# One fused kernel, a TensorE product shared by two blocks on row halves, and a new order of its steps

## The chip, the cores and the metric

The kernel runs on one core of one Trainium2 chip. The metric is the device time of one execution in microseconds (us). TensorE (PE) does the matmuls, and its weight loads are shown apart (PEld); VectorE (DVE), ScalarE (ACT) and GpSimd (POOL) do the elementwise work; SyncE (SP) issues the transfers.

## The reference, cut to what matters

Three layers follow one another: an mLSTM-like attention over gates (2 batches, 8 heads, 768 rows, head size 40), a mixture of four attention experts, and a mixer. The change touches mostly the last stage of the mixer, which is called the channel stage here:

```
xt = x.transpose(0, 2, 1)
h = np.maximum(xt @ w_tok1, 0.0) @ w_tok2
u = x + h.transpose(0, 2, 1)
h2 = np.maximum(u @ w_ch1, 0.0) @ w_ch2      # 320 -> 1536 -> 320
return (u + h2).astype(np.float32)
```

## The kernel before

All three layers are one program. The work is cut into parts, Python generators that stop at each step; `ORDER` is a list of numbers written out ahead, and each number runs the next step of one part on one engine (part number times 5 plus the engine: PE, ACT, DVE, POOL, SP). So the order of every engine's queue is that list; a negative number -n puts n small filler matmuls on PE (`fillers`, tile `still`). The conditions that a part yields (`on(...)`) are checked when the list is played at build time; on the chip an engine waits only where data or a buffer needs it.

Gates are scanned along the sequence on DVE, then each of 12 chunks (2 batches of 6) of 128 rows goes through `m_rows` (a tile `rt` of stabiliser rows), `m_products` (tag pd), `m_whole` (scores, 40-row products), `m_scores`, `m_carry`, `m_intra`, `m_update`. The first two chunks' `rt` are made by a multiply (four ACT operations or one on DVE); from the third on two small DMAs fill them. Then come the experts (`p_qk`, `p_v`, `a_scores`, `a_unit`, `a_value`, `a_tail`), the token stage (`t_hidden`, `t_mix`, `c_turn`) and the channel stage.

Every product that needs precision is a sum of hi and lo halves in fp32r. In the channel stage the 320 inputs are two blocks of 128 rows and one of 64 that stands twice, on rows 0 to 63 and 64 to 127. `c_hidden(k, g)`, for 12 blocks k of 128 hidden columns and 3 groups g of 512 rows, runs `kpass`: three products for each of the first two blocks and two for the third, eight of 128x512 in all, into one PSUM bank. In the third block the hi weights stand on the upper rows and their lo part on the lower, so hi times x_hi and lo times x_hi are one product; the eighth is the same weights by x_lo. ACT then writes h hi (relu), DVE h lo, both into tiles of the tag `e`, and `c_out(k, g)` runs four times three products of 128x320 into four accumulator banks (tile `cw` is a weight block, `h` its input). There are eight PSUM banks.

Weights of the channel stage come as 64-bit floats: `narrow` loads one (tile `raw`), narrows it with three DVE operations, one ACT operation ahead of them and one behind, and DVE writes the lo half (`cw`). A block k from 6 on can only be loaded when a place (`home`) is free; blocks 8 to 11 take those that `c_out` of blocks 0 to 3 gives back with the last group (`cwused`).

Of the kernel before, what the change touches and what calls it, by code (L numbers as in the profile page):

```python
# [39 lines left out]
EARLY = 4  # L40
STOP = -1000
# [14 lines left out]
    937, 422, 524, 895, 187, 508, 432, 900, STOP, 560, 917, 187, 440, 488, 936, 896, 387, 440, 561, 901, 1482, 530,  # L56
# [1175 lines left out]
```

## Time and profile before

| | us |
|---|---|
| median of 3 runs | 334.23 |
| lowest, highest | 334.22, 334.96 |
| profiled execution: its time | 334.46 |
| its span, first to last instruction | 332.7 |

Some 1.76 us of the profiled execution lie outside the span. Busy time of an engine is the union of its instructions, which overlap: a start-to-start time is shorter than an instruction's own duration. PE's ends are modelled, so short waits of PE can hide in its busy time.

### The profile page before, as it was taken

To read this page: it belongs to the slowest core of one execution; us is meant where nothing else is said; L and a number is where in the kernel's file an instruction comes from. 1 tells how busy PE (TensorE), PEld (TensorE's weight loads), DVE (VectorE), ACT (ScalarE), POOL (GpSimd) and SP (SyncE) were. 2 spreads that over 40 slices of the span, in tenths; PEclk is the share of its full clock that TensorE was granted. 3 is DMA by queue.
4 is the path that set the end of the run, shared out by engine and by line. 5 is a ranking of instruction groups with operands and counts; after the bars stand their busy time and mean duration, and the time that the engine had idled before them with its cause. 6 is when DMAs were issued, how large, how long until landed. Compare 5 with 4: busy or idle time off the path is not lost.

```text
span 332.7 us, 7751 instructions
## 1 busy us (share of the span) xinstructions
PE 326.1 (98%) x3034; PEld 293.8 (88%) x3034; DVE 243.1 (73%) x674; ACT 179.4 (54%) x453; POOL 43.3 (13%) x82
## 2 busy tenths in 40 slices
PE   8999999999989999999999999999999999999995
PEld 7779989898888989988899899999889989889985
DVE  4999999999999999999997636543535886411413
ACT  7997769787938886678685513311213442211110
POOL 4232443031421000011120010000000000000000
PEclk9999999999999999999999999999999999999999
DMA  7962844540300354121011502000101200100302
GB/s 228 394 225 97 304 157 153 216 155 13 144 0 3 128 175 144 49 87 41 2 42 48 164 12 89 0 0 2 47 0 41 87 1 2 39 2 0 104 16 79
DMA packets 10300, 29.05 MB, mean 87 GB/s; under 512 B 1272, under 2 KB 3224, under 8 KB 10264
## 3 DMA queue, kind: packets, MB, share of 16 engines
q1 hardware_dynamic: 10120, 28.54, 24.8%
q8 instruction: 24, 0.39, 0.5%
q14 instruction: 12, 0.10, 0.1%
q10 hardware_dynamic: 144, 0.02, 0.0%
HBM read 26.50 MB, written 1.97 MB: 86 GB/s over the span
## 4 chain that ended last, share of the span: by engine, by line
PE 57%; DVE 32%; ACT 4%; issue 3%; DMA 2%; SPq 0%; POOL 0%; DVEq 0%; POOLq 0%; ACTq 0%
PE bank L195 52%; DVE am L864 3%; PE bank L881 3%; DVE e L587 3%; DVE tf L477 3%; DVE tf L474 2%; DMA gt<-in_dram 2%; DVE cw L219 1%; DVE w L222 1%; DVE tf L472 1%; DVE xt L677 1%; ACT am L870 1%; DVE x L222 1%; PE bank L625 1%; DVE q L763 1%
## 5 line engine op out<-in xcount | busy, mean ns | idle before, releaser
L195 PE MATMUL bank<-ut,cw 128*128 128x512 f32 x288 | 72.4, 395 | 0.0
L195 PE MATMUL bank<-cw,h 128*128 128x320 f32 x432 | 70.6, 310 | 0.0
L195 PEld LDWEIGHTS bank<-cw,h 128*128 128x128 f32 x432 | 66.0, 188 | 2.7 <-issue 0.2
L1044 ACT ACTIVATE h<-bank 128x512 fp32r<-128x512 f32 x36 | 21.6, 600 | 78.4 <-PE bank L195 78.3
L195 PEld LDWEIGHTS bank<-ut,cw 128*128 128x128 f32 x288 | 52.6, 188 | 9.8
L1046 DVE SCALAR_TENSOR_TENSOR h<-bank,h 128x512 fp32r<-128x512 f32 x36 | 24.8, 689 | 48.4 <-ACT h L1044 48.4
L870 ACT ACTIVATE am<-am,mn 128x128 f32<-128x128 f32 (+5 forms) x48 | 32.1, 671 | 11.0 <-DVE mn L867 6.6
L864 DVE CUSTOM_DVE_ANT_0 am<-bank,mk 128x384 f32<-128x384 f32 (+3 forms) x64 | 30.6, 500 | 0.8 <-PE bank L195 0.7
L195 PE MATMUL bank<-xt,wh 128*128 128x256 f32 x144 | 26.6, 290 | 0.0
L881 PE MATMUL bank<-ident,am 128*128 128x128 f32 x168 | 24.8, 275 | 0.0
L195 PE MATMUL bank<-ks,q 64*128 64x384 f32 (+2 forms) x192 | 22.4, 343 | 1.1 <-DVE q L763 1.0
L469 ACT ACTIVATE tf<-raw 128x384 f32<-128x384 f32 (+1 forms) x32 | 17.1, 535 | 11.4 <-DVE cw L219 6.0
L216 ACT COPY atr<-bank 128x384 f32<-128x384 f32 (+3 forms) x53 | 22.2, 442 | 2.0 <-PE bank L881 1.9
L195 PEld LDWEIGHTS bank<-xt,wh 128*128 128x128 f32 x144 | 21.8, 189 | 1.0 <-issue 0.2
L195 PE MATMUL bank<-atr,vg 128*64 128x128 f32 x336 | 22.2, 277 | 0.0
L881 PEld LDWEIGHTS bank<-ident,am 128*128 128x128 f32 x168 | 19.4, 140 | 1.8 <-issue 0.3
L195 PEld LDWEIGHTS bank<-atr,vg 128*64 128x64 f32 x336 | 18.4, 137 | 2.1 <-issue 0.6
L195 PEld LDWEIGHTS bank<-ks,q 64*128 64x128 f32 x192 | 15.8, 185 | 4.9 <-DVE q L763 1.2
L477 DVE SCALAR_TENSOR_TENSOR tf<-raw,minus,tf 128x384 uint32<-128x384 uint32 (+1 forms) x32 | 19.1, 595 | 0.2
L474 DVE SCALAR_TENSOR_TENSOR tf<-raw,tf 128x384 uint32<-128x384 uint32 (+1 forms) x32 | 17.5, 556 | 0.3
L1070 DVE TENSOR_TENSOR u<-bank,u 128x320 f32<-128x320 f32 x24 | 11.0, 486 | 8.5 <-PE bank L195 8.5
L587 DVE TENSOR_TENSOR e<-bank,e 128x512 f32<-128x512 f32 x24 | 16.2, 682 | 0.1
(160 smaller groups left out, 601.5 us busy)
## 6 DMA issues: line engine op xcount, KB each, us to landing
kv<-in_dram SPq DMA_DIRECT2D x11, 848.0 KB
raw<-in_dram SPq DMA_DIRECT2D x20, 384.0 KB
raw<-in_dram SPq DMA_DIRECT2D x13, 320.0 KB
os<-in_dram SPq DMA_DIRECT2D x4, 480.0 KB
out_dram<-u SPq DMA_DIRECT2D x12, 160.0 KB
raw<-in_dram SPq DMA_DIRECT2D x3, 386.0 KB
kv<-in_dram SPq DMA_DIRECT2D x1, 512.0 KB
gt<-in_dram SPq DMA_DIRECT2D x1, 512.0 KB
```

The lines of the kernel that those rows point to most:

```text
L195: PE.matmul(o, lt, r, start=first, stop=last)
L216: (A.copy if e == "A" else V.tensor_copy)(o, i)
L469: A.activation(t, w[:, :, 1].bitcast(F32), AF.Copy, scale=2.0 ** -112)
L474: V.scalar_tensor_tensor(u, w[:, :, 0], 29, u, op0=OP.logical_shift_right, op1=OP.bitwise_or)
L477: V.scalar_tensor_tensor(t.bitcast(U32), w[:, :, 1], minus.bitcast(U32), u, op0=OP.bitwise_and, op1=OP.bitwise_or)
L587: V.tensor_mul(EE[n, u], PS[n][u], EE[n, u])
L864: V.tensor_tensor_reduce(a[:, b0 * 128:b1 * 128], s["p", e, ci], mks, -0.125, 3e38, OP.add, OP.min, s["mn"][:, ci, e:e + 1])
L870: A.activation(a[:, 0:w], a[:, 0:w], AF.Exp, bias=s["mn"][:, z, e:e + 1], scale=-1.0, accum_out=s["sm"][:, 0, e:e + 1])
L881: PE.transpose(pt[:, k - b0], a[:, k * 128:(k + 1) * 128], ident)
L1044: A.activation(h[0], p1, AF.Relu)
L1046: V.scalar_tensor_tensor(h[1], p1, 0.0, f32(h[0]), op0=OP.max, op1=OP.subtract)
L1070: V.tensor_add(uo(b, i), ACC[h, n // 4][n % 4], uo(b, i))
```

## The change

- `c_hidden` keeps seven products. The eighth is left to a new part `c_last`, for two blocks k and k+1 of one group together: one product on rows 0 to 63 for block k, one on rows 64 to 127 for k+1, each into its own bank. For that, `narrow` writes the lo half of an odd block's third part on the upper rows in place of the lower ones. The lo-by-lo term of the third block, which the old eighth product held, falls away.
- relu and the lo half become a part of their own, `c_split`, after `c_last`; its tiles come from the pool `big` in place of `e`.
- `DIRECT = 3`: the third chunk's `rt` is made by a multiply; its copy and its two DMAs fall away, and the fifth chunk, which takes the same buffer, gets the copy.
- `m_products`, `m_whole` and `a_tail` yield other conditions for the order list (no wait on the chip).
- `ORDER` is a new list. As it is read against the parts, it has `c_last` 18 times in nine runs of one to three pairs, 58 fillers in runs of 19, 18, 11, 10 (before 80, of 19, 49, 2, 2, 8), and counted by kind takes 25 steps from DVE and gives it 12 of other engines.

```diff
+DIRECT = 3
...
-        if n > 1 and (n < 4 or c < 2):
+        if n >= DIRECT and (n < DIRECT + 2 or c < 2):
             yield on("AV", "sml", *free)
             copy(plan.eng, rt(n), sel(n, True))
-        if n > 1:
+        if n >= DIRECT:
...
         if rem:
-            sub(plan.eng, hi[64:128, m:], t[64:128, m:], f32(hi[64:128, m:]))
+            low = slice(0, 64) if home[1] % 2 else slice(64, 128)
+            sub(plan.eng, hi[low, m:], t[low, m:], f32(hi[low, m:]))
...
     def c_hidden(k, g):
-        yield on("P", ..., take=["bank", "e", "e"])
+        yield on("P", ..., take=["bank"])
         ws = NAR["c1", k]
-        p1 = bank([128, 512])
-        kpass(p1, lambda w, xx, blk, r: (ws[w][r, 128 * blk:128 * blk + 128], UT[g][xx][r, blk]))
+        P1[k, g] = bank([128, 512])
+        for n, (w, x, blk) in enumerate(((0, 0, 0), (1, 0, 0), (0, 1, 0), (0, 0, 1), (1, 0, 1), (0, 1, 1), (0, 0, 2))):
+            mm(P1[k, g], ws[w][:, 128 * blk:128 * blk + 128], UT[g][x][:, blk], n == 0, False)
+        mark(("hd", k, g))
+
+    def c_last(k, g):
+        yield on("P", ("hd", k, g), ("hd", k + 1, g))
+        for u in range(2):
+            r = slice(64 * u, 64 * u + 64)
+            mm(P1[k + u, g], NAR["c1", k + u][0][r, 256:384], UT[g][1][r, 2], False, True)
...
+    def c_split(k, g):
+        yield on("A", ("hp", k - k % 2, g), take=["big"])
+        p1 = P1[k, g]
+        h = H2[k, g] = two(big([128, 2, 512], F32R, "h2"))
         A.activation(h[0], p1, AF.Relu)
```

## Rows read from the trace of the kernel before

**Rows 1.** The page: span, busy time by engine, shares of the chain that ended last.
```profile
span 332.7 us, 7751 instructions
PE 326.1 (98%) x3034; PEld 293.8 (88%) x3034; DVE 243.1 (73%) x674; ACT 179.4 (54%) x453; POOL 43.3 (13%) x82
...
PE 57%; DVE 32%; ACT 4%; issue 3%; DMA 2%; SPq 0%; POOL 0%; DVEq 0%; POOLq 0%; ACTq 0%
```
**Rows 2.** The chain that ended last: start us, us, what.
```profile
2.17 6.06 DMA gt<-in_dram
...
12.14 0.60 DVE e L587
...
92.43 10.38 PE bank L195 x120
...
164.17 0.41 DVE u L1002
164.63 3.60 PE bank L195 x49
...
235.44 92.53 PE bank L195 x515
328.00 1.81 DVE u L1070 x4
```
**Rows 3.** Stretches of 10 us: busy us per engine (instructions), granted clock, DMA share, GB/s.
```profile
0.00:10.00 10.00, 8.96 (x90) 7.54 (x90) 5.62 (x16) 7.50 (x18) 3.76 (x17) 1.00 0.77 261
...
50.00:60.00 10.00, 9.92 (x138) 9.25 (x139) 9.90 (x29) 8.25 (x22) 3.46 (x6) 1.00 0.53 189
...
150.00:160.00 10.00, 10.00 (x85) 8.80 (x85) 9.82 (x33) 8.86 (x26) 1.34 (x2) 1.00 0.13 34
...
300.00:310.00 10.00, 10.00 (x58) 9.07 (x57) 1.86 (x4) 1.80 (x3) 0.00 (x0) 1.00 0.00 0
```
**Rows 4.** Timeline, PE in the channel stage: start us, us, instruction.
```profile
240.67 2.00 PE L195 MATMUL bank<-ut,cw 128*128 128x512 f32 x8
...
242.51 1.92 PE L195 MATMUL bank<-cw,h 128*128 128x320 f32 x12
...
244.27 2.01 PE L195 MATMUL bank<-ut,cw 128*128 128x512 f32 x8
```
**Rows 5.** Timeline, PE around three runs of row-half pairs; in brackets the idle before.
```profile
66.93 0.80 PE L195 MATMUL bank<-ks,q 64*128 64x384 f32 x6
67.66 1.09 PE L195 MATMUL bank<-atr,vg 128*64 128x128 f32 x16
...
75.53 0.94 PE L195 MATMUL bank<-ks,q 64*128 64x512 f32 x6
76.39 0.79 PE L195 MATMUL bank<-cb,w 128*64 128x82 f32 x16
...
174.97 0.31 PE L195 MATMUL bank<-up,tw 128*128 128x320 f32 x1
175.21 0.19 PEld L195 LDWEIGHTS bank<-ks,q 64*128 64x128 f32 x2 [0.19 <-issue]
175.21 1.31 PE L195 MATMUL bank<-ks,q 64*128 64x384 f32 x12
176.46 0.71 PE L195 MATMUL bank<-up,tw 128*128 128x320 f32 x3
```
**Rows 6.** Groups of DVE by form: xcount | busy us, mean ns | idle before.
```profile
L1046 DVE SCALAR_TENSOR_TENSOR h<-bank,h 128x512 fp32r<-128x512 f32 x36 | 24.8, 689 | 48.4 <-ACT h L1044 48.4
...
L587 DVE TENSOR_TENSOR e<-bank,e 128x512 f32<-128x512 f32 x24 | 16.2, 682 | 0.1
...
L222 DVE TENSOR_TENSOR x<-os,dn 128x320 f32<-128x320 f32 x9 | 5.3, 586 | 0.1
...
L216 DVE CAST ut<-bank 128x384 fp32r<-128x384 f32 x6 | 3.3, 546 | 0.0
L216 DVE COPY u<-bank 128x320 f32<-128x320 f32 x6 | 2.9, 483 | 4.1 <-PE bank L195 4.1
...
L219 DVE TENSOR_TENSOR yh<-c,yh 128x256 fp32r<-128x256 f32 x3 | 1.2, 407 | 0.2 <-ACT yh L934 0.2
```
**Rows 7.** Timeline of the start, all engines.
```profile
3.99 4.16 PE L195 MATMUL bank<-still 128*128 128x128 bf16 x49
...
6.35 2.45 ACT L379 ACTIVATE rt<-ms,smlt 128x128 fp32r<-128x128 f32 x8
...
8.08 0.50 PE L195 MATMUL bank<-rt,ms 64*128 64x512 f32 x2
8.32 0.69 DVE L327 TENSOR_TENSOR_SCAN gt<-zz,gt 128x256 f32<-128x256 f32 x1 [0.89 <-DMA gt<-in_dram]
```
**Rows 8.** Timeline around the last weight block: its home comes free, conversion ends, first use.
```profile
256.92 1.92 PE L195 MATMUL bank<-cw,h 128*128 128x320 f32 x12
...
258.67 0.63 PE L195 MATMUL bank<-ut,cw 128*128 128x512 f32 x2
...
280.08 1.26 DVE L219 TENSOR_TENSOR cw<-tf,cw 128x256 fp32r<-128x256 f32 x3
282.17 2.01 PE L195 MATMUL bank<-ut,cw 128*128 128x512 f32 x8
```

More of the change, by code (lines that the diff above doesn't have):

```diff
@@ L40 @@
 EARLY = 4
+DIRECT = 3
 STOP = -1000
 ORDER = [
[11 rows of a table removed]
-    937, 422, 524, 895, 187, 508, 432, 900, STOP, 560, 917, 187, 440, 488, 936, 896, 387, 440, 561, 901, 1482, 530,
[67 rows of a table removed]
[11 rows of a table added]
+    39, 387, 900, 940, 936, 1482, 497, 1486, 901, 1487, 386, 917, 440, 440, 186, 503, 31, 947, 19, 897, 952, STOP,
[68 rows of a table added]
 ]
@@ L362, in m_rows @@
         free = (("mg", n - 2),) if n > 3 else ()
-        if n > 1 and (n < 4 or c < 2):
+        if n >= DIRECT and (n < DIRECT + 2 or c < 2):
             yield on("AV", "sml", *free)
             copy(plan.eng, rt(n), sel(n, True))
-        if n > 1:
-            yield on("S", ("msp", c), *free, *((("rti", n - 1),) if n > 2 else ()))
+        if n >= DIRECT:
+            yield on("S", ("msp", c), *free, *((("rti", n - 1),) if n > DIRECT else ()))
             for u in range(2):
@@ L530, in m_products @@
             for u in range(2):
-                yield on("P", "idb", *((("mg", n - 1),) if n else ()), take=["bank"])
+                yield on("P", "idb", *((("pd", n - 1),) if n else ()), take=["bank"])
                 PD[n].append(bank([128, 4, L]))
                 mm(PD[n][u], identb, negb[:, None, :].to_broadcast([128, 4, L]), True, False)
-        yield on("P", ("rt", n), ("lt", c), *((("mg", n - 1),) if n else ()), take=["e"] * 2 if early else ["bank", "e"] * 2)
+        yield on("P", ("rt", n), ("lt", c), *((("pd", n - 1),) if n else ()), take=["e"] * 2 if early else ["bank", "e"] * 2)
         if not early:
@@ L567, in m_whole @@
     def m_whole(n):
-        yield on("P", ("kv" if n else "kq", n), ("pd", n), take=["bank"] * 2)
+        yield on("P", ("kv" if n else "kq", n), *((("ps", n - 1),) if n else ()), take=["bank"] * 2)
         PS[n] = [bank([128, 4, L]) for _ in range(2)]
@@ L951, in a_tail @@
         mark(("u0", b, i))
-        yield on("AV", take=["big"] * (1 - i % 2))
+        yield on("AV", *((("up", b, i - 1),) if i % 2 else ()), take=["big"] * (1 - i % 2))
         if i % 2 == 0:
@@ L1028, in c_turn @@
         mark(("ut", b, i))
-    H2, ACC = {}, {}
+    H2, ACC, P1 = {}, {}, {}
     TURNS = [(h * HALF + k, g) for h in range(2) for g in range(3) for k in range(HALF)]
@@ L1034, in c_hidden @@
     def c_hidden(k, g):
-        yield on("P", *[("ut", *divmod(4 * g + i, NCH)) for i in range(4)], ("cw", k), *((("hd", *BEFORE[k, g]),) if k or g else ()), take=["bank", "e", "e"])
+        yield on("P", *[("ut", *divmod(4 * g + i, NCH)) for i in range(4)], ("cw", k), *((("hd", *BEFORE[k, g]),) if k or g else ()), take=["bank"])
         ws = NAR["c1", k]
-        p1 = bank([128, 512])
-        kpass(p1, lambda w, xx, blk, r: (ws[w][r, 128 * blk:128 * blk + 128], UT[g][xx][r, blk]))
-        if k == NK - 1:
-            give("big", 2)
-        mark(("hd", k, g))
-        h = H2[k, g] = [work.tile([128, 512], F32R, name="h2", tag="e", bufs=EB) for _ in range(2)]
-        yield on("A")
+        P1[k, g] = bank([128, 512])
[7 more added lines that the diff above has]
+            mm(P1[k + u, g], NAR["c1", k + u][0][r, 256:384], UT[g][1][r, 2], False, True)
+        if k == NK - 2:
+            give("big", 2)
+        mark(("hp", k, g))
+    def c_split(k, g):
+        yield on("A", ("hp", k - k % 2, g), take=["big"])
+        p1 = P1[k, g]
+        h = H2[k, g] = two(big([128, 2, 512], F32R, "h2"))
         A.activation(h[0], p1, AF.Relu)
@@ L1061, in c_out @@
                 mark(("done", k // HALF, 4 * g + i))
-        give("e", 2)
+        give("big")
         mark(("co", k, g))
@@ L1155, in fused_kernel @@
                 add(c_hidden(k, g))
+                if k % 2:
+                    add(c_last(k - 1, g))
+                add(c_split(k, g))
                 add(c_out(k, g))
```

157 rows, old and new, of the table ORDER are left out of this document.

## The prediction, made before the changed kernel ran

> **What bounds the kernel now.** I read the page first. PE is busy for 98% of the span, yet DVE holds 32% of the chain that ended last [rows 1]; so one of the two hides the other. The chain in order of time separates them [rows 2]: it begins with the transfer of the gates, runs mostly over DVE up to 164.6 us (with a stretch of PE from 92 to 120), and is PE alone from 164.63 to 328.0; then come four stores' additions and the last transfer. The windows say the same [rows 3]: up to about 180 DVE is busy 9.8 of 10 us and PE 9.9 or more, and at 300 DVE has 1.9. So there are two halves with two prices. In the second, every microsecond of PE work taken away comes off the end as long as nothing else takes its place. In the first, DVE sets the pace with PE close behind, and PE's waits are hidden in its modelled busy time. The granted clock is full in all windows shown, so it gives nothing.
>
> **The eighth product.** Eight products of 128x512 start at 240.67 and the next group at 242.51; again 244.27 follows twelve of 128x320 begun at 242.51 [rows 4]. So a 512-wide product costs 1.84/8 = 0.230 us, a 320-wide one 1.76/12 = 0.147. The old eighth products cost 36 x 0.230 = 8.28 us.
>
> In their place stand 18 pairs. What a pair of 64-row products costs is seen where the experts' scores do the same, each product of a pair into its own bank. A run of six products, 384 wide, takes 67.66 - 66.93 = 0.73 us to the next start, a run of twelve takes 176.46 - 175.21 = 1.25 [rows 5]. Three pairs more cost 0.52, so a pair costs 0.173; one after the other, six products would have taken over 6 x 0.147 = 0.88, since each is wider than 320. The halves do run together. For 512 columns I add 128 columns at (0.230 - 0.147)/192 each, 0.055: a pair costs 0.23, as much as one full product. 18 x 0.23 = 4.14, so the pairs alone give back 8.28 - 4.14 = 4.14 us.
>
> But a run has a fixed price. 0.73 - 3 x 0.173 = 0.21 lies in the run and its end; its start comes 0.24 after that of the last full product, which alone takes 0.147: 0.09 more, and the weight load there shows 0.19 idle with no other engine to blame [rows 5]. Together 0.30 a run, and there are nine: 2.7 us. The 512-wide run from 75.53 to 76.39, which comes after products of the same half-row kind and so shows only its end, gives 0.86 - 3 x 0.23 = 0.17 as the low bound; for the high one the whole 0.19 idle of the weight load stands for the start, 0.21 + 0.19 = 0.40. For nine runs 1.5 to 3.6. I take 2.7: the rows with both ends are nearest.
>
> The Trainium skill has this as a rule that speaks against the change: "TensorEngine Tiling (Array Packing)", section Key Properties, says that a change of tiling mode drains the engine, whereas tiles work independently. It gives no price for the drain. The trace agrees, with 0.30 us per run; without the drain the sum would be 2.7 us lower. In the same page's section Gotcha 1, row tiles must not share a bank; here each half has its own, as in the scores.
>
> Fewer runs elsewhere: by the lists, half-row runs other than the new ones go from 30 to 26. At 0.30 that is 1.2 us of PE, nearly all in the first half, where DVE leads; I count nothing for it and keep it for the low end.
>
> **What waits on the pairs.** relu and the lo half can now only begin when the second block of a pair and its run are done. Between a pair's end and the first `c_out` that reads it, the new list has at least 2.0 us of other PE work, mostly 4 to 12; ahead of it stand the two operations of a block, some 1.3 us (DVE's takes 0.689 [rows 6]), and for the tightest ones some 2 to 3 us of DVE's queue. In the list of before the least is 1.76, and PE does not stand still in it [rows 4]. So no wait is counted. Up to six banks hold open sums in place of one or two; the four accumulators' banks come from the stores of the group before, and the list puts products of other blocks in front. Bound: 0 to 1 us.
>
> The moved lo half of odd blocks is the same instruction on other rows: nothing. Tiles from `big` in place of `e`: no instruction. What `c_last` leaves out costs nothing.
>
> **The third chunk's rows.** Two small transfers and one copy go from that chunk; a multiply (four ACT operations of 0.39 to 0.6 each [rows 7]) takes their place, and the copy serves the fifth chunk. ACT is not on this chain, and the multiply lies in the first 20 us. The fillers go from 49 ahead of the first `pd` to 18 and one `m_whole`: the 49 run from 3.99 to 8.15, `rt` of the first two chunks is written from 6.35 to 8.80, and `pd` starts at 8.08 [rows 7]. Up to half a microsecond of that is PE's own filler. But DVE's next scan begins at 8.32 since its gates land then, and that transfer keeps its place. I count nothing at the start, bounds -0.5 to +0.5.
>
> **The order in the first half.** Counted by kind, DVE loses 25 steps and gets 12. It loses 5 products `x` (0.586), 5 copies `u` (0.483), 3 casts `ut` (0.546), 4 steps on the weights `c` (about 0.42), two evictions of 0.55, and six smaller ones: 12.2 us in all. It gets 5 `yh` (0.407), two casts of 0.55, a product of some 0.7 and four smaller ones: 5.0 us [rows 6]. The net is 7.2 us of own durations. On the chain a step counts for less: `e` takes 0.682 but moves the chain by 0.60 [rows 2, 6], so 13 steps fewer give 13 x 0.08 = 1.0 less: 6.2 us. About nine tenths of it lies ahead of 165 us by the list. How much reaches the end? Of the first 164.6 us, DVE has 32% of 332.7 = 106 less the last 1.8, so 104.7 us, or 64% of the chain [rows 1, 2]. I take 64% of 6.2 = 4.0. Bounds: nothing, if PE or ACT (8 to 9 of 10 there [rows 3]) takes over at once, and 6.2.
>
> **The sum.** -4.14 + 2.7 - 4.0 = -5.4 against the profiled execution's 334.46, which is 0.23 above the median: 334.23 - 5.4 = 328.8 us. The measurement tells 0.3%, 1.0 us, from no change. The second half alone gives -1.4, the first -4.0.
>
> **Rivals.**
> *PE takes all the relief.* DVE's 6.2 us come through whole and a run costs 0.17: -4.14 + 1.5 - 6.2 = -8.8, 325.4 us. For it: the first half loses four half-row runs and 22 fillers too; against it, PE has at most some tenths of a microsecond in ten to give [rows 3].
>
> *The new order gives nothing in the first half.* 334.23 - 1.4 = 332.8. For it: PE is busy 9.9 of 10 there; against it: the chain is DVE's.
>
> *The pairs do not overlap.* 36 halves at 0.23 save nothing and the runs cost 2.7: 334.23 + 2.7 - 4.0 = 332.9. Rows 5 speak against it.
>
> *Weights late at the last block (slower).* Its home comes free with the last `c_out` of block 3, at 258.67; its lo half is ready at 281.34 and used at 282.17, 23.5 us later [rows 8]. In the new list only 13.9 us of PE work lie between the two: three blocks' seven products at 1.61 each, one pair, and twenty steps of `c_out` at 0.441. If the conversion takes 22.7 us as now, PE waits 8.8: 328.8 + 8.8 = 337.6. It decides from 13.9 + 5.4 = 19.3 us. For it: DVE's queue between the two holds 29 steps of some 16.2 us by their rows, 13.8 on the chain, so there is no room. Against it: in the trace the lo half was done only 0.8 us ahead of its use because nothing hurried it; DVE's queue held other work.
>
> **Chances.** The forecast, 326 to 332, 0.61; all the relief 0.09; nothing in the first half 0.14; no overlap 0.04; late weights, in whole or in a good part, 0.12. Of the two cases near 333, most fall over the bound of 1.0 us and some within it: faster 0.61 + 0.09 + 0.11 = 0.81, same 0.07, slower 0.12. The range leaves out most of the late weights and the far side of the full relief: 325.5 to 333.6; its ends are the low bounds together and the case with nothing from the first half and the dearest runs, 334.23 - 4.14 + 3.6 = 333.7.
>
> **What would show it.** Pairs: groups of 64x512 products `ut`, `cw`, 36, in nine runs; to the next start 0.23 a pair plus 0.2, and about 0.24 between the last full product's start and theirs. 252 full ones at 0.230. DVE's busy time near 237, and the point from which the chain is PE alone some 4 us before 164.6. Fillers 58. PE idle ahead of the 512-wide products between 245 and 275 would mean late weights; waits of the 320-wide ones on DVE's `h`, a split that is late. The forecast is wrong if PE's stretch behind DVE's last entry is not near 162 us (now 163.4), or if that entry does not move.

## The result, and the profile after

The changed kernel takes 330.19 us (median of 4 runs, 329.34 to 331.84) against 334.47 for the kernel before: a ratio of 0.9879, 95% interval 0.9856 to 0.9901, so 1.2% faster. The forecast was 328.8 us, with a range of 325.5 to 333.6. In a later run, the control of the experiments, the same kernel gave 329.27 us and 0.9849 (0.9837 to 0.9862).

The page of the changed kernel, its lines as in [rows 1]:

```profile
span 328.4 us, 7681 instructions
PE 321.0 (98%) x3012; PEld 287.3 (88%) x3012; DVE 234.9 (72%) x661; ACT 182.9 (56%) x463; POOL 46.4 (14%) x86
...
PE 72%; DVE 16%; ACT 5%; issue 3%; DMA 2%; POOL 1%; SPq 0%; DVEq 0%; POOLq 0%
```

The span is 4.3 us shorter. DVE has 8.2 us less busy time (234.9 us, the forecast had some 237) and its share of the chain is halved; PE's has grown from 57% to 72%, though its busy share has not moved. The chain in order of time, as in [rows 2]:

```profile
2.20 6.32 DMA gt<-in_dram
...
105.96 0.70 DVE e L590
106.71 6.20 PE bank L197 x148
...
218.38 105.27 PE bank L197 x586
323.67 1.81 DVE u L1084 x4
```

The last long DVE stretch of the chain now ends at 106.7 us, where it ended at 164.6 [rows 2]. From there PE sets the pace, at its 98%. That says who is in charge, not what was gained: for the gain a mark is needed that both kernels pass. The product of `a_tail` for the fourth block of the second batch is one; the timeline of PE has it in the kernel before at

```profile
169.20 1.04 PE L195 MATMUL bank<-wo,yh 128*128 128x320 f32 x6
```

and in the changed kernel at

```profile
165.64 1.13 PE L197 MATMUL bank<-wo,yh 128*128 128x320 f32 x6
```

Ahead of the mark PE runs the same products in both kernels, but for 22 fillers and three products `up`, `tw` fewer and five products `ident`, `am` more, so the mark is a fair one. 3.56 us come from ahead of it. From the mark to the last additions it was 328.00 - 169.20 = 158.8 us [rows 2] and is 323.67 - 165.64 = 158.0: 0.8 us come from the channel stage and what overlaps it. The forecast had 4.0 and 1.4.

The pairs, in the groups of PE (xcount | busy us, mean ns | idle before) of the changed kernel:

```profile
L197 PE MATMUL bank<-ut,cw 128*128 128x512 f32 x252 | 62.3, 396 | 0.0
L197 PE MATMUL bank<-ut,cw 64*128 64x512 f32 x36 | 6.6, 443 | 0.0
```

and a run of them in its timeline:

```profile
272.89 7.33 PE L197 MATMUL bank<-ut,cw 128*128 128x512 f32 x32
...
278.93 0.39 PE L197 MATMUL bank<-ut,cw 128*128 128x512 f32 x1
...
279.48 0.19 PEld L197 LDWEIGHTS bank<-ut,cw 64*128 64x128 f32 x2 [0.36 <-issue]
...
280.14 3.78 PE L197 MATMUL bank<-cw,h 128*128 128x320 f32 x24
283.77 1.78 PE L197 MATMUL bank<-ut,cw 128*128 128x512 f32 x7
```

This run has two pairs. The group of 32 (28 whole products, four halves) takes 280.14 - 272.89 = 7.25 us. The whole product before the last one begins at 278.93, the last 0.23 later at 279.16, the run at 279.48: 0.09 more than a whole product lasts. From 279.48 to 280.14 the two pairs and their end take 0.66, 0.20 more than 2 x 0.23. That is 0.29 for the run, as forecast from [rows 5]. Reckoned in this way, the nine runs cost 0.28 to 0.31 each, 2.66 us together, for 2.7 forecast. ("About 0.24 between the last full product's start and theirs" in the prediction holds behind a 320-wide product; behind a 512-wide one it is 0.32 here.) The two idle gaps of the weight load at a run's ends (0.36 here) are the sign by which runs are found. The forecast stopped looking at 280.14, though, and the experiments show what that left out.

### The profile page after: what moved, and what is told of

Same layout as the page of the kernel before. It is cut to its first block, busy times and chain, and to the rows that moved or that the text cites. A ratio compares the mean times of both kernels' runs of the same rounds, so it can differ in the third digit from the quotient of the medians.

```text
span 328.4 us, 7681 instructions
## 1 busy us (share of the span) xinstructions
PE 321.0 (98%) x3012; PEld 287.3 (88%) x3012; DVE 234.9 (72%) x661; ACT 182.9 (56%) x463; POOL 46.4 (14%) x86
## 4 chain that ended last, share of the span: by engine, by line
PE 72%; DVE 16%; ACT 5%; issue 3%; DMA 2%; POOL 1%; SPq 0%; DVEq 0%; POOLq 0%
PE bank L197 66%; PE bank L884 4%; DVE am L867 2%; DMA gt<-in_dram 2%; DVE e L590 2%; PE bank L628 1%; ACT e L551 1%; DVE w L224 1%; DVE x L666 1%; DVE tf L479 1%; PE bank L909 1%; DVE tf L476 1%; DVE ks L766 1%; DVE xt L680 1%; DVE u L1084 1%
## 5 line engine op out<-in xcount | busy, mean ns | idle before, releaser
L197 PE MATMUL bank<-ut,cw 128*128 128x512 f32 (+1 forms) x288 | 68.2, 402 | 0.0
L197 PE MATMUL bank<-cw,h 128*128 128x320 f32 x432 | 67.7, 311 | 0.0
L197 PEld LDWEIGHTS bank<-cw,h 128*128 128x128 f32 x432 | 64.2, 188 | 2.3 <-issue 1.7
L197 PEld LDWEIGHTS bank<-ut,cw 128*128 128x128 f32 (+1 forms) x288 | 49.1, 187 | 13.4 <-issue 3.6
L1058 ACT ACTIVATE h<-bank 128x512 fp32r<-128x512 f32 x36 | 19.0, 606 | 46.9 <-PE bank L197 46.9
L1060 DVE SCALAR_TENSOR_TENSOR h<-bank,h 128x512 fp32r<-128x512 f32 x36 | 23.5, 684 | 28.8 <-ACT h L1058 28.8
L197 PE MATMUL bank<-xt,wh 128*128 128x256 f32 x144 | 25.9, 287 | 0.1
L197 PE MATMUL bank<-ks,q 64*128 64x384 f32 (+2 forms) x192 | 20.8, 339 | 0.1
L482 ACT CAST cw<-tf 128x320 fp32r<-128x320 f32 (+1 forms) x24 | 11.6, 488 | 7.6 <-DVE tf L479 7.4
```

The costliest lines, as they stand in the source:

```text
L197: PE.matmul(o, lt, r, start=first, stop=last)
L482: A.copy(hi, t)
L1058: A.activation(h[0], p1, AF.Relu)
L1060: V.scalar_tensor_tensor(h[1], p1, 0.0, f32(h[0]), op0=OP.max, op1=OP.subtract)
```

## The experiments

Times are medians, ratios are to the kernel before on the same chip. A difference to the changed kernel is the one to its control run, by the medians where both ran on one chip and by the ratios otherwise.

**Control.**

> The changed kernel as it is, for comparison on the same chip. Both theories: a ratio near 0.988, 330.2 us.

329.27 us, ratio 0.9849 (0.9837 to 0.9862). A little better than at first; the next three runs were made beside it. The mark and the last additions stand in its trace at

```profile
164.80 1.12 PE L197 MATMUL bank<-wo,yh 128*128 128x320 f32 x6
```

```profile
322.80 1.81 DVE u L1084 x4
```

By this trace 169.20 - 164.80 = 4.4 us come from ahead of the mark, and again 0.8 from behind it (158.0 us). The two traces of the changed kernel part in the first 30 us: one ACT step of the chain (`ks`) starts at 29.58 us in the first and at 28.77 here. So the share of the first half is 3.6 to 4.4 us; from the mark on, the two agree within 0.04.

**Whole products in place of the pairs.**

```diff
         for u in range(2):
-            r = slice(64 * u, 64 * u + 64)
-            mm(P1[k + u, g], NAR["c1", k + u][0][r, 256:384], UT[g][1][r, 2], False, True)
+            mm(P1[k + u, g], NAR["c1", k + u][0][:, 256:384], UT[g][1][:, 2], False, True)
```

> The changed kernel and its order, but each last product of a pair is a whole one over 128 rows, as before the change (the lo-by-lo term comes back for most blocks). My theory (in the channel stage PE alone sets the pace; 36 whole products of 0.232 us stand against 18 pairs of 0.23 and nine runs of 0.30): 8.35 - 6.84 = 1.5 us slower than the changed kernel, near 331.7, ratio 0.992. Rival (the gain is all in the order, the pairs only move PE's time about): within 0.5 us of the changed kernel. Rival (a run costs little, 0.1): 3.3 us slower.

330.19 us, ratio 0.9877 (0.9864 to 0.9889): 0.92 us slower than the control, whose runs all lie lower (329.05 to 329.56 against 329.83 to 330.59). The pairs do earn something, but less than 1.5; and the kernel without them is still 4.1 us faster than before. The same stretch in its PE timeline tells why:

```profile
272.65 7.60 PE L197 MATMUL bank<-ut,cw 128*128 128x512 f32 x32
280.09 3.69 PE L197 MATMUL bank<-cw,h 128*128 128x320 f32 x24
283.61 1.78 PE L197 MATMUL bank<-ut,cw 128*128 128x512 f32 x7
```

The 32 products take 7.44, so the run of two pairs saves 0.19 there, as the step had it (4 x 0.23 less 0.75). But the 24 products behind it take 283.61 - 280.09 = 3.52 us here and 3.63 with the pairs. A run of half-row products costs another 0.1 us in the whole products that follow it. The other traced places agree: where 320-wide products follow a run (five places), the second starts 0.25 to 0.26 us after the first and twelve take 1.86 to 1.89; with whole last products at the same places these are 0.15 and 1.76 to 1.77. So a run costs about 0.39, not 0.30.

**Halves that can't overlap.**

```diff
-            r = slice(64 * u, 64 * u + 64)
+            r = slice(0, 64)
```

> The changed kernel, but both halves of a pair use rows 0 to 63, so that the two can't run side by side; for odd blocks the product then takes the lo weights by x_lo in place of hi by x_lo. My theory (the halves run together, 0.23 a pair): now 0.46 a pair, 18 x 0.23 = 4.1 us slower than the changed kernel, near 334.3, ratio 1.000. Rival (the halves hardly overlap as it is): no more than 1 us slower.

333.44 us, ratio 0.9978 (0.997 to 0.9986): 4.17 us slower than the control, for 4.1 expected. So the two halves of a pair run fully side by side when they stand on different rows, and not when they share them.

**One pair to a run.**

```diff
 # in the order list, for each pair:
-... c_hidden(k, g), c_hidden(k + 1, g), others, c_last(k, g), c_last(of another pair) ...
+... c_hidden(k, g), c_hidden(k + 1, g), c_last(k, g), others ...
```

> The changed kernel, but each pair stands right behind the seventh product of its second block, so 18 runs of one pair in place of nine of one to three. My theory (0.30 us for each run): 9 x 0.30 = 2.7 us slower, near 332.9, ratio 0.996. Rival (the price is in the pair, not in the run): same as the changed kernel, or a little faster, since relu can begin earlier.

332.68 us, ratio 0.9953 (0.994 to 0.9966): 3.41 us slower than the control, for nine more runs: 0.38 each. That is the price of the run above from another side. With it, single pairs alone would lose: 36 whole products cost 36 x 0.232 = 8.35, 18 single runs 18 x (0.23 + 0.38) = 11.0.

**More fillers at the start.**

```diff
-ORDER: ... 18 fillers, m_whole of chunk 0, pd of chunk 0 ...
+ORDER: ... 49 fillers, m_whole of chunk 0, pd of chunk 0 ...
```

> The changed kernel with the second run of fillers at 49, as before the change, in place of 18: 31 small products more on PE ahead of the first score products. My theory (at the start DVE's scan waits for the gates' transfer till 8.3 to 8.6 us, so PE has room): at most 0.5 us slower than the changed kernel, 330.2 to 330.7. Rival (PE sets the pace from the start, so that fewer fillers were a good part of the gain in the first half): 31 x 0.08 = 2.5 us slower, 332.7.

329.5 us, ratio 0.9843 (0.9805 to 0.988): no difference to the control's 0.9849 that can be told. PE has room there.

**Fourteen steps back on DVE.**

```diff
-m_intra xo (chunks 1, 4, 6, 7, 9): POOL;  a_tail u (5 blocks): ACT
-a_scale c (2 blocks): POOL;  a_scale copy (2 blocks): ACT
+all fourteen: DVE, at the same places of the order list
```

> The changed kernel with 14 of its steps back on DVE in place of ACT and POOL (five products x, five copies u, two weights c, two evictions of c), all else and the order as they are: some 7.0 us of DVE's own durations, 5.9 on the chain. My theory (DVE set the pace in the first half and its relief gave the gain there): 3 to 6 us slower than the changed kernel, 333 to 336. Rival (with the new order PE sets the pace from 107 us on and DVE has room): 1 us slower or less.

333.16 us, ratio 0.9951 (0.9928 to 0.9974): 1.0% above the control's ratio, 3.4 us. The mark comes 3.3 us later than in the control:

```profile
168.10 1.13 PE L195 MATMUL bank<-wo,yh 128*128 128x320 f32 x6
```

DVE has 14 instructions more and 4.4 us more busy time than in the changed kernel, and its share of the chain is back where it was before the change:

```profile
PE 323.3 (98%) x3012; PEld 287.6 (87%) x3012; DVE 239.3 (72%) x675; ACT 180.6 (55%) x456; POOL 42.5 (13%) x79
...
PE 56%; DVE 33%; ACT 3%; issue 3%; DMA 3%; SPq 0%; DVEq 0%; ACTq 0%
```

**The same fourteen steps taken off DVE in the kernel before.**

```diff
-the same fourteen steps: DVE
+m_intra xo, a_scale c: POOL;  a_tail u, a_scale copy: ACT
```

> The kernel before with the same 14 steps moved off DVE to ACT and POOL, order unchanged. My theory (DVE sets the pace till 165 us): 64% of 5.9, 3.8 us faster than before, 330.7, ratio 0.989. Rival (the moves alone do little, it is the search of the order that uses them; ACT and POOL get waits of their own): within 1 us of before, or slower.

333.53 us, ratio 0.9964 (0.994 to 0.9989): 0.4% faster than before, 1.2 us by the ratio and 0.7 by the medians (the kernel before had 334.25 beside it), not 3.8. My theory named the right engine, and yet the relief alone brings a fifth to a third. The page's chain shows where the rest stays:

```profile
PE 88%; DVE 7%; DMA 2%; issue 1%; ACT 1%; SPq 0%; DVEq 0%
```

and so does the mark in PE's timeline:

```profile
167.62 1.05 PE L193 MATMUL bank<-wo,yh 128*128 128x320 f32 x6
```

DVE has all but left the chain (7%), and PE took it over at once: in this profiled execution, with 332.93 us one of the faster ones, the mark comes 1.6 us earlier than before the change. With the new order it stands at 165.64 and 164.80, 2.0 to 2.8 us earlier still. So the order of before leaves PE more time ahead of that mark, for nearly the same products.

**The third chunk's multiply in the kernel before.**

```diff
-        if n > 1 and (n < 4 or c < 2):
+        if n >= 3 and (n < 5 or c < 2):
...
-        if n > 1:            # two small transfers
+        if n >= 3:
```

> The kernel before with the third chunk's rows by a multiply (four ACT operations where its two transfers stood, the copy moved to the fifth chunk), all else as before. My theory: the start is held by the gates' transfer and DVE, so no difference beyond 0.5 us, 334.0 to 335.0. Rival (the wait for the two small transfers stood on the chain of the first 20 us): 1 to 2 us faster, 332.5 to 333.5.

336.23 us, ratio 1.005 (1.0028 to 1.0072): 2 us slower. Neither theory had that. The chain of the start shows the multiply on it, in the middle of a stretch that ACT now sets:

```profile
13.65 0.74 ACT wh L433
14.39 1.18 ACT rt L378 x4
15.63 0.89 ACT os L403
```

**The two transfers again in the changed kernel.**

```diff
-DIRECT = 3
+DIRECT = 2      # in the order list: the copy to ACT's start, the transfers where the multiply stood
```

> The changed kernel with the third chunk's rows by a copy and two small transfers again, in the places where the copy of the fourth chunk and the multiply stand; the fifth chunk's copy falls away. Theory (the multiply lengthens ACT's chain at the start whatever the order, as it cost 2 us in the order of before): 1 to 2 us faster than the changed kernel, ratio 0.980. Rival (the new order has made room for it, PE sets the pace later anyway): within 0.7 us of the changed kernel, or slower, since nothing was arranged for the transfers' wait.

336.45 us, ratio 1.0054 (1.0036 to 1.0072): 7 us slower than the changed kernel, and slower than the kernel before. PE's waits (us, times, longest) and the chain begin the story:

```profile
PE bank L195 <- DMA rt<-ms: 3.1, 1, 3.1
```

```profile
12.27 4.31 DMA rt<-ms
```

and the windows of its start, with columns as in [rows 3], end it:

```profile
10.00:15.00 5.00, 3.66 (x76) 3.27 (x73) 4.93 (x12) 3.05 (x6) 1.64 (x4) 1.00 1.01 407
15.00:20.00 5.00, 3.29 (x21) 2.41 (x23) 2.65 (x8) 2.32 (x5) 0.46 (x1) 0.59 0.94 328
20.00:25.00 5.00, 5.00 (x74) 4.78 (x72) 2.19 (x4) 1.62 (x4) 1.15 (x2) 0.50 0.26 96
25.00:30.00 5.00, 5.00 (x64) 4.03 (x63) 3.51 (x8) 3.85 (x10) 0.95 (x2) 0.88 0.55 175
```

The transfers are 4 KB each, but their issue is at 12.27, when the DMA engines are full with 407 GB/s of keys, values and weights, and it takes 4.3 us from there until what PE waits for has landed. PE stands still for 3.1 us. Then its granted clock falls to 0.59 and 0.50, the lower of its two levels (1.2 GHz), and is back at the upper one before 30 us: some 10 us at half speed, going by the three windows' means. In the changed kernel the third chunk's `pd` runs at 13.99 without a wait, and in the kernel before it ran at 17.54, as the two timelines of PE have it:

```profile
13.99 0.49 PE L197 MATMUL bank<-rt,ms 64*128 64x512 f32 x2
```

```profile
17.54 0.50 PE L195 MATMUL bank<-rt,ms 64*128 64x512 f32 x2
```

**Broken runs and a control for them.**

```diff
             ps = [bank([128, wm]) for _ in range(2)]
+            if (b, i, j, ci) in BROKEN:      # 13 steps behind another half-row step
+                mm(ps[0][:, 0:128], still, still, True, True)
```

> The changed kernel with one small whole product (bf16, 128 columns, into a bank that the next product overwrites) put in front of 13 of the experts' score steps between 85 and 175 us, each of which follows another half-row step: 13 runs of half-row products more, and 13 small products. My theory now (PE sets the pace there with the new order, and a run costs 0.38): 13 x (0.38 + 0.08) = 6 us slower than the changed kernel, near 335, ratio 1.003. Rival (DVE sets the pace there, PE has room): 1 us slower or less.

332.58 us, ratio 0.9947 (0.993 to 0.9964): 3.3 us slower than the control, by the medians (the kernel before had 334.38 beside it and 334.34 beside the control).

```diff
         pu = bank([128, DM])
+        mm(pu[:, 0:128], still, still, True, True)      # in t_mix, 12 steps
```

> Control for the run before: the same small product 12 times, but ahead of the token stage's second products, which are whole products themselves, so that no run is added. My theory: 12 x 0.08 = 1.0 us slower than the changed kernel at most, ratio 0.988. Rival (any product more costs as much, by its place in PE's queue): as much as the run before.

330.33 us, ratio 0.989 (0.9862 to 0.9917): about 1.1 us, 0.09 for each product, so PE does set the pace there. What is left, 3.3 - 1.1 = 2.2 us, is 0.17 for a broken run, under half of the 0.38. Beside the control's trace, PE's products start 0.15 to 0.37 us later from each of the 13 steps on, small product included, and 0.35 of it is made up again at 105.9 us, where the chain is DVE's. The rest of the gap stays: the price is smaller than in the channel stage, and why is open. The rival of the first of the two runs (no more than 1 us) falls, and so does that of the control (as much as the other).

**Whole products for the two single pairs.**

```diff
-            r = slice(64 * u, 64 * u + 64)
+            r = slice(64 * u, 64 * u + 64) if (k, g) not in ((0, 0), (8, 0)) else slice(0, 128)
```

> The changed kernel, but the two runs that hold a single pair take whole products (the lo-by-lo term comes back for those four). My theory (a run costs 0.38, a single pair saves 0.464 - 0.23 = 0.23): 2 x 0.15 = 0.3 us faster than the changed kernel, ratio 0.984; at the edge of what five rounds tell. Rival (a run costs 0.2 or less): same or slower.

329.08 us, ratio 0.9844 (0.9824 to 0.9864): the fastest median of all, but not to be told from the changed kernel's 0.9849. The trace tells more:

```profile
164.63 1.13 PE L197 MATMUL bank<-wo,yh 128*128 128x320 f32 x6
```

```profile
322.59 1.81 DVE u L1084 x4
```

From the mark to the last additions it is 157.96 us, and 158.00 in the control: 0.04 of the 0.3 expected. Beside the control's trace, the starts of PE's products show where the rest went. The second single pair, at 265.8 us with whole products behind it, had cost 0.15 us more than two whole products, as a run of 0.38 has it. The first, at 183.4 us with products of the form 128*64, as the lines print it, behind it (`atr`, `vg`), had cost 0.08 less. There the form changes with or without the pair; that this is the reason was not shown.

## Why the prediction was right, point by point

**What bounds the kernel.** Right for the kernel before: two halves with two prices, DVE ahead in the first, PE close behind. Steps given back to DVE cost 3.4 us; twelve small products more on PE cost 1.1. For the changed kernel the picture was wrong by the prediction's own sign: DVE's last entry should have come some 4 us earlier, with PE's stretch behind it near 162 us. The entry moved from 164.6 to 106.7, by 58 us, and the stretch is 323.67 - 106.71 = 217 us. DVE's chain gave way much further than the time did, since PE stood close behind it.

**The eighth product.** The mechanism is shown: the halves overlap in full (4.17 us when they can't, for 4.14), and what eats the gain is a fixed price per run. The term that was mis-sized is the run's: 0.30 in the forecast, 0.38 measured by nine more of them. The forecast closed the run's account at the start of the next product, and up to there it was right; the 0.1 us between the first and the second product behind the run was not in the sum. The price lies near the forecast's high bound of 0.40. With 0.38, 8.35 - 4.14 - 9 x 0.38 = 0.8, and 0.92 was measured. The Trainium skill's rule ("TensorEngine Tiling (Array Packing)", Key Properties) is that a change of tiling mode drains the engine. The trace agrees in so far as each of the nine runs pays; that it is a drain, no run here shows apart from the price.

**The first half.** The sum was near (4.0 for 3.6 to 4.4), but that is in part luck. "64% of DVE's relief" about holds when it is taken back from the new order (3.4 us of some 5.9), not when it is given to the old one: there 0.7 to 1.2 us come, because PE takes over the chain. What made up for it was counted at nothing: the new order reaches the mark 2.0 to 2.8 us ahead of the relief alone (167.62 against 165.64 and 164.80). With the relief alone PE holds 88% of the chain, so this part is put down to PE's time, which is argued; which of the order's changes gave it was not settled. Fillers at the start are not the cause (no difference for 31 more). Fewer changes of form are a candidate: ahead of the mark PE's products stand in 94 stretches of one form before and in 77 after, 29 and 24 of them on half rows. Five half-row runs at 0.17 to 0.38 are 0.9 to 1.9 us, argued and not shown.

**The third chunk's rows.** Counted at nothing, and that step was wrong in both directions. In the old order, where the two transfers were issued from 11.78 us on and `pd` came at 17.54, the multiply and the moved copy cost 2 us, with the multiply on ACT's chain. In the new order `pd` of that chunk comes 3.6 us earlier, at 13.99, and the multiply saves 7 us against two transfers put in its place, for which nothing else was arranged. The forecast asked what hides the multiply, but not what the new order would do without it.

**Rivals.** The late weights did not come. The timeline of the changed kernel has the conversion of the last weight block that `c_hidden` reads end at 269.5 us,

```profile
268.72 0.75 DVE L221 TENSOR_TENSOR cw<-tf,cw 128x256 fp32r<-128x256 f32 x2
```

and its first product comes seven behind 272.89, at about 274.5; though the window shows DVE at its limit there:

```profile
260.00:270.00 10.00, 10.00 (x60) 8.87 (x59) 9.63 (x23) 5.02 (x12) 0.00 (x0) 1.00 0.00 0
```

PE has no idle time ahead of those products but the runs' own. "Nothing in the first half" is refuted by the fourteen steps given back to DVE, "no overlap" by the halves on the same rows. "PE takes all the relief" (325.4 us) did not come either: it wanted DVE's 6.2 us whole and a run at 0.17. What partly came is the other bound of the first half, that PE takes over: it is the chain from 106.7 us on, and that limited the gain.

## What to carry to other kernels

Products on row halves have to earn their run: a pair saves one product's time (0.23 us here), a run among whole products costs 0.38, so there a single pair loses, two just pay, and three earn. A step that is priced at nothing in the old order can hold up the new one; before it is called free, ask what would wait in the new order if it were gone. And where two engines are both near their limit, relief of one is worth only what the other has left: 0.7 to 1.2 us in the old order, 3.4 in the new one.

## What had not been expected of the hardware

Two transfers of 4 KB took 4.3 us from the first issue to landing while the queues moved 407 GB/s. The wait of 3.1 us on PE that they caused was followed by some 10 us at half the granted clock, and the run ended 7 us later. And the price of a half-row run is partly paid behind it: 0.1 us of it shows only between the starts of the first and the second whole product that follow.
